# One of eight pairs of a fused attention and FFN kernel computes h with seven half-width block products

## The chip, the core and the metric

The kernel runs on one core of one Trainium2 chip. The metric is device time in microseconds (us) of one launch; lower is better. The engines are named as the profile names them: PE (matrix products; PEld are its weight loads), DVE and ACT (elementwise work), SP (which issues the DMAs here), POOL (idle here). Each engine takes its instructions strictly in the order of its own queue, so an instruction that waits holds up everything queued behind it on its engine.

## The reference

```python
def _attn_ref(q, k, v, tau):                     # q, k, v: (4, 6080, 256)
    qn = q / (norm(q, axis=1, keepdims=True) + 1e-06)
    kn = k / (norm(k, axis=1, keepdims=True) + 1e-06)
    s = kn.transpose(0, 2, 1) @ qn / tau         # (4, 256, 256): over channels
    s = s - s.max(-1, keepdims=True)
    a = exp(s)
    a /= a.sum(-1, keepdims=True) + 1e-09
    return v @ a

def _moe_ref(x, w_in, w_out):                    # x: (24320, 256), w_in: (256, 2048), w_out: (2048, 256)
    h = maximum(x @ w_in, 0.0)
    return h * h @ w_out
```

The output is `_moe_ref` of the attention's output, reshaped to 24320 tokens.

## The kernel before, in words

**What is computed.** The attention matrix `a` of a batch is only 256x256, so the kernel folds it into the weights: `W = a @ w_in`, once per batch, and then `h = relu(v W)`, squares it and multiplies with `w_out`. Every fp32 operand of a product is split into a high and a low float32r part (`..._hi` by a copy on ACT, `..._lo` by a subtraction on DVE), and each product is three: hi·hi, hi·lo, lo·hi.

**Tiles and steps.** A batch has 12 blocks of tokens, ten of 512 and two of 480 (`blocks`, line 75). A block has 16 steps, one for each 128 hidden columns (f), and two steps make a pair r (8 pairs). `first_product` (line 574) makes one step's h: six products of 512 columns into a bank of `ps_h` (three banks, line 98), and ACT evicts it through Relu into half of the tile `x`. After the odd step ACT squares `x` in place (`squares_and_sums`, line 598).

**The second product by seven.** For all blocks but the first two and the last, `h² @ w_out` uses the Strassen-Winograd scheme: over a pair and the two halves of the tokens it needs 7 block products of 256 columns (times 3 parts, 21 matmuls) in place of 8. It costs sums: three DVE operations on `x` (`x<-x`, 512, 256 and 256 elements) and two more slices in `g_hi`/`g_lo`, which hold the seven operands' parts: 768 elements of plain `x` (in `squares_and_sums`) and 1024 elements of sums (`parts_of_sums`, line 611, one step later). `g_hi` is ACT's, `g_lo` is DVE's. PE uses pair r's parts two pairs later (LAG, line 793): 9 matmuls in the even step (the 768-element parts), 12 in the odd step (`SEVEN`, line 641). When a block's eighth pair is through, ACT copies the results out of `ps_o` (`o<-ps_o`), and `combine` (line 681) adds them up on DVE at the next block's steps 5, 7 and 9.

**What runs beside it.** v of the next block is loaded (`load_v`), and split on ACT at step 6 and on DVE at step 8. The attention of the next batch runs as a generator (`attention`, line 370), one piece per step: a chunk of q and k is split in one even step (`qk_hi`, `qk_lo`), squared and added up in the next (`qk`, `acc`), and its products follow on PE (`gram`). It is skipped in steps 2 and 3 of a block (line 815). Its softmax and the new W (`softmax_and_W`, line 402) follow.

**Order.** The main loop (lines 795 to 843) writes out each step by hand: first product, generators in even steps, `parts_of_sums`, `squares_and_sums`, a piece of `combine`, second product, v's loads and splits, generators in odd steps. `InProgramOrder` keeps that order on each engine, so every instruction shows line 27 in the profile and has to be told by its tiles.

Of the kernel before, what the change touches and what calls it, by code (L numbers as in the profile page):

```python
# [30 lines left out]
def kernel(  # L31
# [25 lines left out]
    P = 128  # L57
# [7 lines left out]
    FPG = GRP // P  # L65
    J = 2
# [167 lines left out]
    now = {"part": 0}  # L234
    HEAD = 5
    QK_BUFS = 2
# [69 lines left out]
    def start_first(b=0):  # L306
# [7 lines left out]
        def load(c):  # L314
            if c == g.n:
                grams[1] = Gram(1)
            if c < g.n:
                g.load(c, FAST_TAGS[c % len(FAST_TAGS)])
            elif c < total and B > 1:
                grams[1].load(c - g.n, raw=room[:, c - g.n] if c - g.n < HEAD - 1 else None)  # L320
# [80 lines left out]

    def softmax_and_W(b):
# [49 lines left out]
        ps_b = ps_h.tile([P, T], F32, tag="h", name=f"ps_b{b}")  # L452
# [17 lines left out]
        ps_t = ps_h.tile([P, T], F32, tag="h", name=f"ps_t{b}")  # L470
# [6 lines left out]
        eT_hi = pool.tile([P, NC, C], F32R, tag="eT_hi", name=f"eT_hi{b}", bufs=1)  # L477
        eT_lo = pool.tile([P, NC, C], F32R, tag="eT_lo", name=f"eT_lo{b}", bufs=1)
# [5 lines left out]
        for g in range(NG):  # L484
# [54 lines left out]
            yield  # L539

# [16 lines left out]
    def once(f, *args):  # L557
        f(*args)
        yield

    def split_v_lo(b, n):
# [3 lines left out]
        vector.tensor_sub(V[b, n][2][:, :, :tn], raw[:, :, :tn], hi[:, :, :tn].bitcast(F32))  # L565

# [6 lines left out]

    def first_product(b, n, f):
        tn = blocks[n][1]
# [22 lines left out]
    def squares_and_sums(b, n, r):  # L598
# [3 lines left out]
        scalar.activation(x[:, 0:4, :], x[:, 0:4, :], AF.Square)  # L602
# [192 lines left out]
    for i in range(len(steps) + 2 * LAG):  # L795
        part = now["part"] = i % 2
        if i < len(steps):
# [26 lines left out]
        if part == 1 and i // 2 < len(pairs):  # L824
            squares_and_sums(*pairs[i // 2])
# [3 lines left out]
        if i >= 2 * LAG:  # L829
            second_product(*pairs[i // 2 - LAG], part)  # L830
        if i < len(steps):
            at_hi, at_lo = (None, None) if at == 0 else (12, 13) if at == 1 else (6, 8)
# [4 lines left out]
            if f == at_lo and at + 1 < len(order):  # L837
                split_v_lo(*order[at + 1])
                if at + 2 < len(order):
                    load_v(*order[at + 2])  # L840
        if i >= PAIR and part:
# [29 lines left out]
```

## Time and profile before

| what | value |
|---|---|
| time, median of 3 runs (range) | 2218.08 us (2217.61 to 2218.21) |
| the profiled execution's own time | 2217.84 us |
| its span | 2216.1 us |
| PE's granted clock | 1.000 |
| DMA, mean over the span | 57 GB/s |

The span is the time from the first to the last instruction of the profiled execution; 1.7 us of the execution's time lie around it. A "busy" PE is a model: matmuls overlap in the records, so their rate is read from the distance between starts. A row of the timeline gives start, duration, engine, operation, tiles (out<-in), the shape, how many equal ones were merged, and in brackets how long the engine stood idle before it and what released it.

### The profile page before, as it was taken

How to read it: one execution, taken by the hardware profiler on the slowest of the kernel's cores; microseconds unless marked ns; L12 is line 12 of the kernel's file. 1: busy time of each engine (PE TensorE's matmuls, PEld its weight loads, DVE VectorE, ACT ScalarE, POOL GpSimd, SP SyncE). 2: the span in 40 equal slices, each digit the busy share in tenths (PEclk: the TensorE clock that was granted, in tenths of full speed). 3: DMA queues.
4: the chain of work that ended last, by engine and by line, in shares of the span. 5: the costliest groups of instructions: out<-in, count | busy, mean ns of one | idle time of the engine just before them, and what ended most of it. 6: DMA issues, size and time to landing. Idle time of an engine off the chain costs nothing.

```text
span 2216.1 us, 34362 instructions
## 1 busy us (share of the span) xinstructions
PE 2204.7 (99%) x13740; PEld 1980.2 (89%) x13740; DVE 1760.9 (79%) x2470; ACT 1844.3 (83%) x2294; POOL 0.7 (0%) x6
## 2 busy tenths in 40 slices
PE   9999999999999999999999999999999999999999
PEld 7788999989989999988998999998899888888898
DVE  7878888888778888878767888887877777777773
ACT  5788888888788888888878888888887888888885
POOL 0000000000000000000000000000000000000000
PEclk9999999999999999999999999999999999999999
DMA  9511122101111122110121222110102010010000
GB/s 341 179 67 48 61 71 61 55 20 36 60 66 58 60 68 65 61 41 22 36 76 48 64 67 71 58 53 22 38 20 76 21 37 20 22 37 20 22 26 18
DMA packets 76495, 126.99 MB, mean 57 GB/s; under 512 B 7728, under 2 KB 35120, under 8 KB 76336
## 3 DMA queue, kind: packets, MB, share of 16 engines
q1 hardware_dynamic: 76336, 124.81, 17.2%
q8 instruction: 107, 1.75, 0.3%
q14 instruction: 52, 0.43, 0.1%
HBM read 95.68 MB, written 29.10 MB: 56 GB/s over the span
## 4 chain that ended last, share of the span: by engine, by line
PE 96%; DVE 1%; ACT 1%; DMA 1%; SPq 0%; issue 0%; DVEq 0%; ACTq 0%
PE ps_h L27 47%; PE ps_o L27 42%; PE gram L27 5%; PE ps_w L27 2%; DVE acc L27 1%; DMA qk<-in_k 1%; DMA qk<-in_q 0%; ACT x L27 0%; PE ps_n L27 0%; DVE g_lo L27 0%; DVE dec_m L27 0%; ACT g_hi L27 0%; DVE x L27 0%; ACT sq L27 0%; SPq L263 0%
## 5 line engine op out<-in xcount | busy, mean ns | idle before, releaser
L27 DVE TENSOR_TENSOR g_lo<-x,g_hi 128x768 fp32r<-128x768 f32 (+2 forms) x744 | 804.1, 1081 | 95.3 <-ACT g_hi L27 94.6
L27 DVE TENSOR_TENSOR x<-x 128x256 f32<-128x256 f32 (+3 forms) x1080 | 550.9, 510 | 277.6 <-ACT x L27 252.3
L27 ACT CAST g_hi<-x 128x768 fp32r<-128x768 f32 (+2 forms) x744 | 697.4, 937 | 25.3 <-DVE x L27 12.7
L27 ACT ACTIVATE x<-ps_h 128x512 f32<-128x512 f32 (+1 forms) x768 | 456.4, 594 | 290.6 <-PE ps_h L27 269.8
L27 PE MATMUL ps_h<-v_hi,w_hi 128*128 128x512 f32 (+1 forms) x1536 | 478.5, 393 | 0.0
L27 PE MATMUL ps_h<-v_hi,w_lo 128*128 128x512 f32 (+1 forms) x1536 | 477.6, 391 | 0.0
L27 PE MATMUL ps_h<-v_lo,w_hi 128*128 128x512 f32 (+1 forms) x1536 | 474.8, 390 | 0.0
L27 ACT ACTIVATE x<-x 128x1024 f32<-128x1024 f32 (+1 forms) x384 | 404.5, 1053 | 11.9
L27 PE MATMUL ps_o<-g_lo,wS_hi 128*128 128x256 f32 (+1 forms) x1440 | 401.7, 279 | 0.0
L27 PE MATMUL ps_o<-g_hi,wS_lo 128*128 128x256 f32 (+1 forms) x1440 | 401.2, 279 | 0.0
L27 PE MATMUL ps_o<-g_hi,wS_hi 128*128 128x256 f32 (+1 forms) x1440 | 400.4, 278 | 0.0
L27 PEld LDWEIGHTS ps_h<-v_lo,w_hi 128*128 128x128 f32 x1536 | 287.9, 187 | 64.9
L27 PEld LDWEIGHTS ps_h<-v_hi,w_lo 128*128 128x128 f32 x1536 | 288.5, 188 | 62.0
L27 PE MATMUL ps_o<-g_hi,wo_hi 128*128 128x256 f32 (+3 forms) x1176 | 330.8, 288 | 1.0 <-ACT g_hi L27 1.0
L27 PE MATMUL ps_o<-g_hi,wo_lo 128*128 128x256 f32 (+3 forms) x1176 | 330.8, 288 | 0.0
L27 PE MATMUL ps_o<-g_lo,wo_hi 128*128 128x256 f32 (+3 forms) x1176 | 330.5, 288 | 0.1
L27 PEld LDWEIGHTS ps_o<-g_lo,wS_hi 128*128 128x128 f32 x1440 | 271.0, 188 | 15.7
L27 PEld LDWEIGHTS ps_o<-g_hi,wS_hi 128*128 128x128 f32 x1440 | 270.3, 188 | 15.5
L27 PEld LDWEIGHTS ps_o<-g_hi,wS_lo 128*128 128x128 f32 x1440 | 270.6, 188 | 0.0
L27 PEld LDWEIGHTS ps_h<-v_hi,w_hi 128*128 128x128 f32 x1536 | 239.0, 188 | 5.2
L27 PEld LDWEIGHTS ps_o<-g_hi,wo_hi 128*128 128x128 f32 x1176 | 221.5, 188 | 17.7 <-ACT g_hi L27 1.4
L27 PEld LDWEIGHTS ps_o<-g_lo,wo_hi 128*128 128x128 f32 x1176 | 220.8, 188 | 16.7 <-DVE g_lo L27 0.5
(87 smaller groups left out, 1669.2 us busy)
## 6 DMA issues: line engine op xcount, KB each, us to landing
qk<-in_k SPq DMA_DIRECT2D x87, 256.0 KB, 2.8
qk<-in_q SPq DMA_DIRECT2D x87, 256.0 KB, 3.0
v<-in_vT SPq DMA_DIRECT2D x40, 512.0 KB, 3.7
out_T<-o SPq DMA_DIRECT2D x152, 128.0 KB, 1.7
wi_hi<-wi_kept SPq DMA_DIRECT2D x12, 512.0 KB, 3.2
wi_lo<-wi_kept SPq DMA_DIRECT2D x12, 512.0 KB, 4.1
w_raw<-in_w_in SPq DMA_DIRECT2D x4, 1024.0 KB, 6.1
w_raw<-in_w_out SPq DMA_DIRECT2D x4, 1024.0 KB, 5.4
```

Of the source, the lines that this page charges most:

```text
L27: return lambda *args, **kwargs: self.tc.keep_in_program_order(issue(*args, **kwargs))
```

## The change

Pair r = 5 (steps 10 and 11) of every block from the fourth on in batch 0, and from the second on in batches 1 to 3 (42 pairs in all), computes h by the same scheme of seven block products, each of half the tokens: 21 matmuls of 256 columns in place of 12 of 512.

- Step 10 makes four of the seven into two banks, `one` and `two` of `ps_h`; ACT copies two of them out (P1, P5), and DVE makes U2 = `one` + P1, adds U2 to both halves of `two` in PSUM, and makes the third sum `x3` = `two` + P5. Step 11 makes the other three products on top of these banks, and ACT evicts: Relu of `x3`, of `one`, of `two`. In the built program the first of the three (into `one`) waits for U2, the other two (into `two`) wait for `x3`; the copy P1 waits until the tile `x` is free, that is for the 1024-element `g_lo` of pair 3.
- In step 11 the second product is issued ahead of the first product. The sums and 768-element parts of pair 4 (`sums_and_parts`) move from step 9 to step 10, behind the new DVE operations.
- The generators are also skipped in step 10. So the attention's pieces for ACT and DVE run in six even steps of a block (0, 4, 6, 8, 12, 14) where it was seven.
- v's sums (three DVE operations, `v_sums`) are made in step 0, ahead of pair 0's sums; their parts in step 3 (ACT, `vS_hi`) and step 6 (DVE, `vS_lo`). The split of the next block's v moves from steps 6 and 8 to 9 and 12, and its load to step 0.
- W's sums for pair 5 are made once per batch (`sums_of_W`, six DVE operations, one ACT copy).
- For memory: w_in's parts share the tag of the q/k chunks (`qk`), eT shares `qk_hi`, and for batches 1 to 3 the softmax's `ps_b` and `ps_t` use the gram's bank in place of one of `ps_h`.

```diff
--- before.py
+++ after.py
...
+    def small_psum(b, name):
+
+        if b:
+            return ps_g.tile([P, NC, C], F32, tag="gram", name=f"{name}{b}").rearrange("p a b -> p (a b)")
+        return ps_h.tile([P, T], F32, tag="h", name=f"{name}{b}")
...
-        ps_b = ps_h.tile([P, T], F32, tag="h", name=f"ps_b{b}")
+        ps_b = small_psum(b, "ps_b")
...
+    SEVEN_FIRST, FIRST = (5,), 3
+    WS = {}
...
+    def sums_of_W(b, r):
+
+        while now["dec"]:
+            yield
+        f0 = 2 * (r % PPG) * P
+        hi, lo = (w[:, :, f0 : f0 + 2 * P].bitcast(F32) for w in W[b, r // PPG])
+        room = pool.tile([P, 2, NC, 2 * P], F32, tag="dec", name=f"w{b}_{r}", bufs=1)
+        w = room[:, 0]
+        S = room[:, 1].rearrange("p j (i m) -> p (j i) m", i=2)
+        vector.tensor_add(w, hi, lo)
+        A11, A12, A21, A22 = (w[:, j, i * P : (i + 1) * P] for i in range(2) for j in range(2))
+        S1, S2, S3, S4 = (S[:, i] for i in range(4))
+        vector.tensor_add(S1, A21, A22)
+        vector.tensor_sub(S3, A11, A21)
+        vector.tensor_sub(S2, S1, A11)
+        vector.tensor_sub(S4, A12, S2)
+        WS[b, r] = [pool.tile([P, 4, P], F32R, tag=f"WS{r}_{p}", name=f"WS_{p}{b}_{r}", bufs=1) for p in ("hi", "lo")]
+        scalar.copy(WS[b, r][0], S)
+        vector.tensor_sub(WS[b, r][1], S, WS[b, r][0].bitcast(F32))
+        yield
...
+    def sums_of_v(b, n):
+        tn = blocks[n][1]
+        half = tn // 2
+        raw = V[b, n][0]
+        S = pool.tile([P, 4, half], F32, tag="dec", name=f"v_sums{b}_{n}", bufs=1)
+        VS[b, n] = [pool.tile([P, 4, half], F32R, tag=f"vS_{p}", name=f"vS_{p}{b}_{n}", bufs=1) for p in ("hi", "lo")]
+        VS[b, n].append(S)
+        B21, B22 = raw[:, 1, 0:half], raw[:, 1, half:tn]
+        vector.tensor_sub(S[:, 0:3:2, :], raw[:, :, half:tn], raw[:, 0, :tn].rearrange("p (k t) -> p k t", k=2))
+        vector.tensor_sub(S[:, 1, :], B22, S[:, 0, :])
+        vector.tensor_sub(S[:, 3, :], B21, S[:, 1, :])
+        now["dec"] = True
+
+    def sums_of_v_hi(b, n):
+        scalar.copy(VS[b, n][0], VS[b, n][2])
+
+    def sums_of_v_lo(b, n):
+        hi, lo, S = VS[b, n]
+        vector.tensor_sub(lo, S, hi.bitcast(F32))
+        now["dec"] = False
...
+        if part == 0:
+            x = X[b, n, r] = pool.tile([P, 8, half], F32, tag="x", name=f"x{b}_{n}_{r}")
+            one, two = H[b, n, r] = [
+                ps_h.tile([P, 2, T // 2], F32, tag="h", name=f"ps_h{b}_{n}_{r}_{i}")[:, :, :half] for i in range(2)
+            ]
+            product(one[:, 0], "A11", "B11", start=True)
+            product(one[:, 1], "S2", "T2", stop=True)
+            product(two[:, 0], "S1", "T1", start=True)
+            product(two[:, 1], "S3", "T3")
+            P1, P5, U2 = (x[:, i, :] for i in (4, 5, 6))
+            scalar.copy(P1, one[:, 0])
+            scalar.copy(P5, two[:, 0])
+            vector.tensor_add(U2, one[:, 1], P1)
+            vector.tensor_add(two, two, x[:, 6:7, :].broadcast_to([P, 2, half]))
+            vector.tensor_add(x[:, 3, :], two[:, 1], P5)
+        else:
+            one, two = H.pop((b, n, r))
+            x = X[b, n, r]
+            product(one[:, 0], "A12", "B21", stop=True)
+            product(two[:, 0], "S4", "B22")
+            product(two[:, 1], "A22", "T4", stop=True)
+            scalar.activation(x[:, 3, :], x[:, 3, :], AF.Relu)
+            scalar.activation(x[:, 0, :], one[:, 0], AF.Relu)
+            scalar.activation(x[:, 1:3, :], two, AF.Relu)
...
-    def squares_and_sums(b, n, r):
+    def squares(b, n, r):
+        x = X[b, n, r]
+        scalar.activation(x[:, 0:4, :], x[:, 0:4, :], AF.Square)
+
+    def sums_and_parts(b, n, r):
...
+        chained, chain_next = (j < len(steps) and first_by_seven(*steps[j]) for j in (i, i + 1))
+        if chained and part:
+            second_product(*pairs[i // 2 - LAG], part)
...
-        if i >= PAIR and steps[min(i, len(steps) - 1)][2] in (2 * LAG - 2, 2 * LAG - 1):
+        if i >= PAIR and (chained and part == 0 or steps[min(i, len(steps) - 1)][2] in (2 * LAG - 2, 2 * LAG - 1)):
             gens = ()
         if i < PAIR or part == 0:
             for gen in gens:
                 next(gen, None)
+        if chained and part == 0:
+            sums_and_parts(*pairs[i // 2 - 1])
         if part == 0 and 0 <= i // 2 - 1 < len(pairs):
             parts_of_sums(*pairs[i // 2 - 1])
         if i in steps_of_W:
             next(first)
         if part == 1 and i // 2 < len(pairs):
-            squares_and_sums(*pairs[i // 2])
+            squares(*pairs[i // 2])
+            if not chain_next:
+                sums_and_parts(*pairs[i // 2])
         if part and late_work:
             if next(late_work[0], "end") == "end":
                 late_work.pop(0)
-        if i >= 2 * LAG:
+        if i >= 2 * LAG and not (chained and part):
             second_product(*pairs[i // 2 - LAG], part)
         if i < len(steps):
-            at_hi, at_lo = (None, None) if at == 0 else (12, 13) if at == 1 else (6, 8)
+            at_hi, at_lo = (None, None) if at == 0 else (12, 13) if at == 1 else (9, 12)
             if i == 2 and len(order) > 2:
                 load_v(*order[2])
             if f == at_hi and at + 1 < len(order):
                 split_v_hi(*order[at + 1])
             if f == at_lo and at + 1 < len(order):
                 split_v_lo(*order[at + 1])
-                if at + 2 < len(order):
+                if at == 1 and at + 2 < len(order):
                     load_v(*order[at + 2])
+            if at > FIRST - 1:
+                if f == 0 and has_sums(b, n):
+                    sums_of_v(b, n)
+                if f == 0 and at + 1 < len(order):
+                    load_v(*order[at + 1])
+                if f == 3 and has_sums(b, n):
+                    sums_of_v_hi(b, n)
+                if f == 6 and has_sums(b, n):
+                    sums_of_v_lo(b, n)
+            if i in (26, 28):
+                next(first, None)```

DVE's queue around pair 5 of block 5 in batch 1, before (the name x1_5_4 is tile `x` of batch 1, block 5, pair 4; g_lo likewise):

```order
L27 TENSOR_TENSOR g_lo1_5_3_8336<-x1_5_3_8308,g_hi1_5_3_8335 128x1024
L27 TENSOR_TENSOR v_lo1_6_8388<-v1_6_7912,v_hi1_6_8325 128x1024
L27 TENSOR_TENSOR x1_5_4_8364<-x1_5_4_8364 128x512
L27 TENSOR_TENSOR x1_5_4_8364<-x1_5_4_8364 128x256 x2
L27 TENSOR_TENSOR g_lo1_5_4_8401<-x1_5_4_8364,g_hi1_5_4_8400 128x768
L27 TENSOR_TENSOR o1_4_8202<-o1_4_8202 128x256
L27 TENSOR_TENSOR o1_4_8202<-o1_4_8202 128x2x256
L27 TENSOR_TENSOR qk_lo2_17_8442<-qk2_17_8244,qk_hi2_17_8441 128x1024
L27 TENSOR_TENSOR g_lo1_5_4_8401<-x1_5_4_8364,g_hi1_5_4_8400 128x1024
L27 TENSOR_TENSOR x1_5_5_8439<-x1_5_5_8439 128x512
```

The same place now (ps_h1_5_5_0 is bank `one`, ps_h1_5_5_1 bank `two`):

```order
L27 TENSOR_TENSOR g_lo1_5_3_8608<-x1_5_3_8573,g_hi1_5_3_8607 128x1024
L27 TENSOR_TENSOR o1_4_8479<-o1_4_8479 128x256
L27 TENSOR_TENSOR o1_4_8479<-o1_4_8479 128x2x256
L27 TENSOR_TENSOR x1_5_5_8687<-ps_h1_5_5_0_8688,x1_5_5_8687 128x256
L27 TENSOR_TENSOR ps_h1_5_5_1_8689<-ps_h1_5_5_1_8689,x1_5_5_8687 128x512
L27 TENSOR_TENSOR x1_5_5_8687<-ps_h1_5_5_1_8689,x1_5_5_8687 128x256
L27 TENSOR_TENSOR x1_5_4_8641<-x1_5_4_8641 128x512
L27 TENSOR_TENSOR x1_5_4_8641<-x1_5_4_8641 128x256 x2
L27 TENSOR_TENSOR g_lo1_5_4_8708<-x1_5_4_8641,g_hi1_5_4_8707 128x768
L27 TENSOR_TENSOR g_lo1_5_4_8708<-x1_5_4_8641,g_hi1_5_4_8707 128x1024
L27 TENSOR_TENSOR x1_5_5_8687<-x1_5_5_8687 128x512
```

The three new operations stand ahead of pair 4's sums, and two pieces of combine ahead of them; `v_lo` is gone from here.

ACT's queue from the eviction of step 3 to that of step 5 of the same block, before:

```order
L27 ACTIVATE x1_5_1_8189<-ps_h1_5_3_8204 128x512
L27 ACTIVATE x1_5_1_8189<-x1_5_1_8189 128x1024
L27 CAST g_hi1_5_1_8212<-x1_5_1_8189 128x768
L27 COPY o1_4_8202<-ps_o1_4_1_7804 128x1024
L27 ACTIVATE x1_5_2_8240<-ps_h1_5_4_8233 128x512
L27 ACTIVATE qk2_15_7959<-qk2_15_7959 128x1024
L27 CAST g_hi1_5_1_8212<-x1_5_1_8189 128x1024
L27 ACTIVATE x1_5_2_8240<-ps_h1_5_5_8265 128x512
```

The same stretch of ACT's queue now:

```order
L27 ACTIVATE x1_5_1_8466<-ps_h1_5_3_8481 128x512
L27 ACTIVATE x1_5_1_8466<-x1_5_1_8466 128x1024
L27 CAST g_hi1_5_1_8490<-x1_5_1_8466 128x768
L27 COPY o1_4_8479<-ps_o1_4_1_8063 128x1024
L27 CAST vS_hi1_5_8418<-v_sums1_5_8417 128x1024
L27 ACTIVATE x1_5_2_8518<-ps_h1_5_4_8511 128x512
L27 CAST qk_hi2_13_8520<-qk2_13_8278 128x1024
L27 CAST g_hi1_5_1_8490<-x1_5_1_8466 128x1024
L27 ACTIVATE x1_5_2_8518<-ps_h1_5_5_8536 128x512
```

`vS_hi` is put in ahead of the eviction of step 4.

More of the change, by code (lines that the diff above doesn't have):

```diff
@@ L319, in load @@
             elif c < total and B > 1:
-                grams[1].load(c - g.n, raw=room[:, c - g.n] if c - g.n < HEAD - 1 else None)
+                last = pool.tile([P, 2, J, C], F32, tag="vS_lo", name="qk_head", bufs=1) if c == total - 1 else None
+                grams[1].load(c - g.n, raw=room[:, c - g.n] if last is None else last)
         for c in range(AHEAD):
```

48 lines of the change are left out of this document (36 added, 12 removed).

## The prediction

> **What bounds the kernel now.** I read the page first: the engines' busy time and the chain that ended last.
>
> ```profile
> PE 2204.7 (99%) x13740; PEld 1980.2 (89%) x13740; DVE 1760.9 (79%) x2470; ACT 1844.3 (83%) x2294; POOL 0.7 (0%) x6
> PE 96%; DVE 1%; ACT 1%; DMA 1%; SPq 0%; issue 0%; DVEq 0%; ACTq 0%
> ```
>
> PE is the bound: the chain lies on it for 96% of the span. The list of waits says the same, since ACT's longest wait in total is for PE:
>
> ```profile
> ACT x L27 <- PE ps_h L27: 269.8, 462, 4.2
> ```
>
> Those 269.8 us are the only reserve that ACT has, and shares of the whole span hide how it is spread. So next come windows of one block each: one beside three chunks of attention, one without attention, one of 480 tokens, and the last block of batch 1, which makes the next W.
>
> ```profile
> core 0: us, PE busy (x) PEld busy (x) DVE busy (x) ACT busy (x) POOL busy (x), PEclk, DMA share, GB/s
> 205.00:251.20 46.20, 46.20 (x302) 41.91 (x302) 39.33 (x52) 41.16 (x50) 0.00 (x0) 1.00 0.18 58
> 1833.80:1875.70 41.90, 41.90 (x267) 37.63 (x266) 32.28 (x47) 35.34 (x44) 0.00 (x0) 1.00 0.08 26
> 1071.30:1111.10 39.80, 39.80 (x266) 36.99 (x265) 30.85 (x47) 33.71 (x43) 0.00 (x0) 1.00 0.09 27
> 1111.10:1158.00 46.90, 46.90 (x296) 42.67 (x296) 33.65 (x52) 35.94 (x48) 0.00 (x0) 1.00 0.20 67
> ```
>
> PE never pauses in them, but beside attention ACT is already busy for 41.2 of 46.2 us and DVE for 39.3.
>
> **What PE gains.** Half-width products are only worth it if they take half the time. PE's timeline, for 512 and 256 columns and for 480 and 240:
>
> ```profile
> 1000.80 0.63 PE L27 MATMUL ps_h<-v_hi,w_hi 128*128 128x512 f32 x2
> ...
> 1002.20 0.28 PE L27 MATMUL ps_o<-g_hi,wo_hi 128*128 128x256 f32 x1
> ...
> 1003.25 0.62 PE L27 MATMUL ps_h<-v_hi,w_hi 128*128 128x512 f32 x2
> ...
> 1089.80 0.59 PE L27 MATMUL ps_h<-v_hi,w_hi 128*128 128x480 f32 x2
> ...
> 1091.09 0.27 PE L27 MATMUL ps_o<-g_hi,wo_hi 128*128 128x240 f32 x1
> ...
> 1092.10 0.59 PE L27 MATMUL ps_h<-v_hi,w_hi 128*128 128x480 f32 x2
> ```
>
> Six products of 512 take 1002.20 - 1000.80 = 1.40 us, 0.233 each; the nine of 256 behind them take 1.05, 0.117 each. Twelve wide ones are 2.80, twenty-one narrow ones 2.45 to 2.46: 0.34 us gained in a pair. At 480 tokens it is 0.215 and 0.112, so 2.58 - 2.36 = 0.22. Of the 42 pairs 34 lie in blocks of 512 and 8 in blocks of 480: 34 x 0.34 + 8 x 0.22 = 13.3 us. No product is added elsewhere on PE.
>
> [...]
>
> **What DVE and ACT pay, step by step.** For each kind of instruction I take the distance from its start to the next one's, in a stretch where the queue never ran dry. DVE:
>
> ```profile
> 1364.35 0.69 DVE L27 TENSOR_TENSOR o<-o 128x512 f32<-128x512 f32 x1
> 1364.95 1.22 DVE L27 TENSOR_TENSOR acc<-acc,qk 128x1024 f32<-128x1024 f32 x1
> ...
> 1367.73 1.61 DVE L27 TENSOR_TENSOR x<-x 128x512 f32<-128x512 f32 x3 [0.43 <-ACT x L27]
> 1369.26 0.95 DVE L27 TENSOR_TENSOR g_lo<-x,g_hi 128x768 fp32r<-128x768 f32 x1
> 1370.13 0.88 DVE L27 TENSOR_TENSOR o<-o 128x256 f32<-128x256 f32 x2
> 1370.92 1.22 DVE L27 TENSOR_TENSOR qk_lo<-qk,qk_hi 128x1024 fp32r<-128x1024 f32 x1
> 1372.06 1.22 DVE L27 TENSOR_TENSOR g_lo<-x,g_hi 128x1024 fp32r<-128x1024 f32 x1
> 1373.19 1.22 DVE L27 TENSOR_TENSOR v_lo<-v,v_hi 128x1024 fp32r<-128x1024 f32 x1
> ...
> 1376.72 1.14 DVE L27 TENSOR_TENSOR o<-o 128x256 f32<-128x256 f32 x2
> 1377.78 1.22 DVE L27 TENSOR_TENSOR acc<-acc,qk 128x1024 f32<-128x1024 f32 x1
> ```
>
> So: a pair's three sums 1.53, `g_lo` of 768 elements 0.87, anything of 1024 elements 1.14, combine 0.60, 0.79 and 1.06 in its three pieces. ACT:
>
> ```profile
> 1352.52 1.04 ACT L27 CAST g_hi<-x 128x1024 fp32r<-128x1024 f32 x1
> 1353.45 0.80 ACT L27 COPY o<-ps_o 128x768 f32<-128x768 f32 x1
> 1354.46 0.60 ACT L27 ACTIVATE x<-ps_h 128x512 f32<-128x512 f32 x1 [0.20 <-PE ps_h L27]
> 1355.09 1.06 ACT L27 ACTIVATE x<-x 128x1024 f32<-128x1024 f32 x1
> 1356.20 0.83 ACT L27 CAST g_hi<-x 128x768 fp32r<-128x768 f32 x1
> 1356.94 1.01 ACT L27 COPY o<-ps_o 128x1024 f32<-128x1024 f32 x1
> 1357.84 0.60 ACT L27 ACTIVATE x<-ps_h 128x512 f32<-128x512 f32 x1
> 1358.33 1.05 ACT L27 CAST qk_hi<-qk 128x1024 fp32r<-128x1024 f32 x1
> 1359.27 1.06 ACT L27 CAST g_hi<-x 128x1024 fp32r<-128x1024 f32 x1
> 1360.22 0.60 ACT L27 ACTIVATE x<-ps_h 128x512 f32<-128x512 f32 x1
> 1360.85 1.06 ACT L27 ACTIVATE x<-x 128x1024 f32<-128x1024 f32 x1
> ```
>
> So: eviction 0.49 or, where the square waits for it, 0.63; square 1.10; 768 elements 0.74; 1024 elements 0.94; the results' copies 0.70 and 0.90. For the new small operations the groups give:
>
> ```profile
> L27 ACT ACTIVATE x<-ps_h 128x512 f32<-128x512 f32 x640 | 383.2, 599 | 224.2 <-PE ps_h L27 204.8 <-DVE g_lo L27 11.4 <-DVE v_lo L27 1.8
> L27 DVE TENSOR_TENSOR x<-x 128x256 f32<-128x256 f32 x608 | 258.5, 425 | 20.8
> L27 DVE TENSOR_TENSOR x<-x 128x512 f32<-128x512 f32 x304 | 210.0, 691 | 196.9 <-ACT x L27 196.4
> L27 DVE TENSOR_TENSOR s<-s,ps_b 128x512 f32<-128x512 f32 x4 | 2.7, 680 | 0.4 <-PE ps_b L27 0.4
> ```
>
> A DVE operation of 512 elements costs the same from PSUM (680 ns) as from SBUF (691). U2, the sum into `two`, and `x3` depend on each other: 0.43 + 0.69 + 0.43 and some 0.03 between them, 1.60 us. No row shows DVE writing PSUM; I take 0.69 for that one and keep up to twice that as the upper end. On ACT a Relu of 256 elements takes some 0.39 (0.60 less 256 elements at 0.85 ns, the slope from 512 to 1024 above), 0.30 to the next start.
>
> In one block that is, on DVE, 1.60 + 1.53 (`v_sums`) + 1.14 (`vS_lo`), on ACT some 2 us. By busy time it fits. But the work is a chain that passes from one queue to the other, so I follow it through one block beside attention, from the end of `x3` (time 0) to the next one's, taking what each queue holds in program order:
>
> 1. DVE makes pair 4's sums (done 1.53), only then can ACT make its 1024-element `g_hi`, and behind that in ACT's queue stand the Relus of `x3`, `one`, `two` and the square: 0.94 + 0.30 + 0.30 + 0.63 + 1.10. Pair 5's sums start at 4.8.
> 2. DVE is then never idle: three pairs' sums and 768-element parts (3 x 2.40), seven operations of 1024 elements (three `g_lo`, `v_lo`, two `acc`, one `qk_lo`: 7.98), `v_sums` 1.53: 16.7. Pair 0's sums start at 21.5 and give their last result at 23.1.
> 3. ACT's 1024-element `g_hi` of pair 0 has waited for that, and what stands behind it follows: `g_hi` 0.94, copy 0.70, eviction 0.63, square 1.10, 768 elements 0.74, copy 0.90, the new `vS_hi` 0.94, eviction 0.49, `qk_hi` 0.94, `g_hi` 0.94, eviction 0.63, square 1.10: 10.05. Pair 2's sums start at 33.2.
> 4. DVE again without a gap: two pairs' sums and 768-element parts 4.80, combine 2.45, five of 1024 elements (`acc`, `g_lo`, `vS_lo`, `qk_lo`, `g_lo`) 5.70, the three new operations 1.60: 14.55. `x3` ends at **47.7**.
>
> PE needs for the same block 46.2 - 0.34 = 45.9 us. `x3` is what the last six products of step 11 wait for, and PE takes its queue in order, so the block lasts 47.7: 1.8 us of waiting in every such pair. In the first one of a batch, where DVE still starts on time, the same steps give a wait of 0.5.
>
> Without attention there is no `acc`, `qk_lo`, `qk_hi`: part 1 is 4.8; in part 2 DVE now waits for ACT between pairs (sums 1.6, `g_hi` 0.94, eviction 0.63, square 1.1, 4.3 a pair; with `v_lo` and `v_sums` between them 14.7, and 1.6 to the last sum); part 3 is 9.1; part 4 is 14.55 - 2.28 = 12.3. That is **42.5** against PE's 41.9 - 0.34 = 41.6: 0.9 us of waiting. At 480 tokens DVE's busy time is 30.85/32.28 = 0.956 of that, so some 40.6 against 39.6: 1.0.
>
> The 42 pairs: 22 beside attention (3 first ones 0.5 = 1.5; 19 at 1.8 = 34.2); 10 in blocks of 512 without attention at 0.9 = 9.0, one more that starts half-way on time, 0.6, and the first of batch 3 with none; 5 of 480 at 1.0 = 5.0; and three that lie in the blocks of 46.9 us, where W's products give PE 7 us of other work, with none. Sum 50.3 us.
>
> **The rest** has one answer. W's sums are about 3 us on DVE three times outside the blocks above, and once in batch 0's first blocks; the 768-element parts are ready some 3.5 us ahead of PE there (they wait two pairs), so nothing. v's load now has steps 0 to 9 for its landing. The shared tags are free before they are asked for: w_in's reload comes after the last chunk. `ps_b` and `ps_t` in the gram's bank take pressure off `ps_h`, where no PE wait is shown now: nothing either way, at most 1 us.
>
> **Sum.** 2217.8 - 13.3 + 50.3 = 2254.8 for the profiled execution, which lies 0.2 us under the median; the forecast for the median is **2255**, 1.7% slower.
>
> **The rivals.**
>
> - *Nothing waits, faster.* If both chains are shorter than PE's block, by 1.8 of 47.7 us (4%) and 0.9 of 42.5 (2%), the pairs gain their 13.3: 2204.8. For it: the three banks of `ps_h` and LAG let the queues run behind for some microseconds, and PE waits nowhere now. Against it: the distances are measured, and a lag that comes back in every block is not absorbed by buffers. Chance 0.18.
> - *Only beside attention.* If part 1 or 3 is a microsecond shorter than I have it, blocks without attention just hold: 2217.8 - 13.3 + 36 = 2240.5. Chance 0.17.
> - *PSUM is dearer on DVE.* If the sum into `two` takes twice as long, `x3` comes 0.7 later in some 36 pairs: up to 2280, middle 2267. Chance 0.13.
> - *Gain and wait cancel.* A quarter of the waits, 13 us: within 0.2%, about 4.4 us and about what a measurement of this kernel can tell from no change. Chance 0.05.
>
> [...]
>
> **How the numbers follow.** The forecast's case, both chains binding, has 0.47. An error of 0.5 us in a block's chain moves its result by 18 us, so its own range is 2237 to 2273. Slower by over 0.2%: 0.47 + 0.17 + 0.13 = 0.77; same 0.05; faster 0.18. The range leaves out the case without waits and the far end of the dear PSUM: 2216 to 2277.
>
> **What would show it.** Right: PE idle before `ps_h` products, released by DVE `x`, once in a block, 1 to 2 us beside attention and under 1 us in batch 3; ACT's waits for PE much below 269.8 us; blocks beside attention near 47.7 us, batch 3's near 42.5. Wrong: blocks of 41.6 us in batch 3 and no wait on PE (the first rival), or a sum into `two` of well over 0.7 us (the third). If PE waited mostly for `g_lo` or for W at a batch's border, the mechanism would be another.

## The result, and the profile after

The changed kernel takes 2274.3 us (median of 4 runs, 2273.4 to 2275.4), the kernel before beside it 2217.85 (2217.6 to 2218.2): a ratio of 1.0255, 95% interval 1.0237 to 1.0272, so 56 us slower. The forecast was 2255, its range 2216 to 2277. The profiled execution of the changed kernel takes 2274.5 us, its span is 2272.7.

From the page of the changed kernel, the engines and the chain that ended last:

```profile
PE 2222.5 (98%) x14118; PEld 1993.4 (88%) x14118; DVE 1926.0 (85%) x2788; ACT 1869.1 (82%) x2466; POOL 0.7 (0%) x6
DVE 47%; ACT 28%; PE 19%; issue 4%; DMA 1%; DVEq 0%; SPq 0%; ACTq 0%
```

The "busy" shares hardly tell the two kernels apart (PE 99% and 98%). The chain does: 96% on PE before, now 75% on DVE and ACT. The list of waits of the changed kernel (us in total, times, longest) says the same from the other side:

```profile
ACT g_hi L27 <- DVE x L27: 244.3, 209, 3.7
...
ACT x L27 <- PE ps_h L27: 76.6, 96, 4.2
...
PE ps_h L27 <- DVE x L27: 21.0, 37, 1.2
```

ACT's reserve, its wait for PE, went from 269.8 to 76.6 us, and ACT now waits for DVE's sums instead. PE waits for DVE's `x` 37 times, 35 of them for `x3` and two for U2. The same four kinds of block as before, in windows of the changed kernel: beside attention, without, the first of 480 tokens in batch 1, and the block behind it, in which half of the next W is made. Blocks are named (batch, block) from here on; these are (2,5), (3,3), (1,10) and (1,11):

```profile
core 0: us, PE busy (x) PEld busy (x) DVE busy (x) ACT busy (x) POOL busy (x), PEclk, DMA share, GB/s
1427.90:1475.60 47.70, 46.74 (x311) 42.29 (x310) 42.53 (x60) 40.97 (x54) 0.00 (x0) 1.00 0.18 56
1885.30:1928.00 42.70, 42.15 (x274) 37.81 (x273) 36.17 (x54) 35.39 (x49) 0.00 (x0) 1.00 0.08 25
1100.80:1143.30 42.50, 41.80 (x284) 38.43 (x283) 37.21 (x60) 34.75 (x53) 0.00 (x0) 1.00 0.08 25
1143.30:1189.40 46.10, 44.69 (x291) 40.64 (x290) 38.58 (x60) 36.31 (x52) 0.00 (x0) 1.00 0.24 80
```

No engine is full in any of them: of DVE and ACT, DVE is the busier and works 42.5 of 47.7 us. Yet every steady block beside attention takes the same 47.7. The prediction's walk can be laid over the timeline of DVE, from the `x3` of block (2,4) (the first row) to that of block (2,5) (the last):

```profile
1411.81 0.42 DVE L27 TENSOR_TENSOR x<-ps_h,x 128x256 f32<-128x256 f32 x1
...
1417.03 1.61 DVE L27 TENSOR_TENSOR x<-x 128x512 f32<-128x512 f32 x3 [0.94 <-ACT x L27]
...
1433.67 1.60 DVE L27 TENSOR_TENSOR x<-x 128x512 f32<-128x512 f32 x3
...
1445.38 1.61 DVE L27 TENSOR_TENSOR x<-x 128x512 f32<-128x512 f32 x3 [0.18 <-ACT x L27]
...
1459.55 0.42 DVE L27 TENSOR_TENSOR x<-ps_h,x 128x256 f32<-128x256 f32 x1
```

`x3` ends at 1412.23. Pair 5's sums start 4.80 later (the walk had 4.8), pair 0's sums end 18.24 after that (18.3), pair 2's sums start 10.11 later (10.05), and `x3` ends 14.59 later (14.55): 47.74, as worked out. Without attention, in batch 3 from the `x3` that ends at 1870.39 to the one at 1913.13, the same four stretches take 4.81, 16.31, 9.16 and 12.46 us (the walk had 4.8, 16.3, 9.1 and 12.3). On PE the end of it is this row, the first of the products into `two` that wait for `x3`:

```profile
1460.12 0.36 PE L27 MATMUL ps_h<-v_hi,WS_hi 128*128 128x256 f32 x1 [0.74 <-DVE x L27]
```

Lengths of blocks of five kernels, from ACT's first eviction in a block to its first in the next (worked out from the timelines); the last three columns are experiments below:

| block | before | after | sums in step 2 | turn in step 10 | all placed anew, W spread |
|---|---|---|---|---|---|
| (2,0), second half of W | 47.19 | 48.09 | 48.09 | 48.11 | 45.92 |
| (2,1), first with the pair | 46.23 | 47.13 | 46.60 | 48.54 | 47.93 |
| (2,4) | 47.68 | 47.74 | 46.58 | 48.90 | 47.17 |
| (2,5) | 46.23 | 47.74 | 46.60 | 48.89 | 46.46 |
| (2,8) | 43.03 | 46.68 | 45.50 | 47.97 | 44.42 |
| (2,9), softmax | 41.55 | 45.30 | 44.86 | 43.77 | 42.02 |
| (2,10), 480 tokens | 39.86 | 42.44 | 41.37 | 40.93 | 39.50 |
| (2,11) | 46.89 | 46.15 | 45.77 | 45.70 | 46.18 |
| batch 2 in all | 546.3 | 562.3 | 551.7 | 567.0 | 545.5 |
| (3,3), no attention | 41.87 | 42.73 | 41.68 | 42.74 | 41.58 |
| (3,10), 480, no attention | 39.86 | 40.90 | 39.82 | 40.91 | 39.63 |

(In the kernel before, blocks alternate because 38 and 46 of gram's products fall into them; in the changed one a steady block has 36, and where attention gets its turn in step 10 back, 42.)

### The profile page after: what moved, and what is told of

Its sections match the earlier page's. It is cut to its first block, busy times and chain, and to the rows that moved or that the text cites. A ratio compares the mean times of both kernels' runs of the same rounds, so it can differ in the third digit from the quotient of the medians.

```text
span 2272.7 us, 35657 instructions
## 1 busy us (share of the span) xinstructions
PE 2222.5 (98%) x14118; PEld 1993.4 (88%) x14118; DVE 1926.0 (85%) x2788; ACT 1869.1 (82%) x2466; POOL 0.7 (0%) x6
## 4 chain that ended last, share of the span: by engine, by line
DVE 47%; ACT 28%; PE 19%; issue 4%; DMA 1%; DVEq 0%; SPq 0%; ACTq 0%
DVE x L27 18%; ACT x L27 13%; DVE g_lo L27 13%; PE ps_h L27 9%; PE ps_o L27 8%; ACT g_hi L27 8%; DVE acc L27 4%; ACT o L27 3%; DVE v_sums L27 2%; DVE qk_lo L27 2%; DVE v_lo L27 2%; DVE vS_lo L27 2%; DVE o L27 2%; PE ps_w L27 2%; ACT vS_hi L27 2%
## 5 line engine op out<-in xcount | busy, mean ns | idle before, releaser
L27 ACT CAST g_hi<-x 128x768 fp32r<-128x768 f32 (+2 forms) x744 | 697.9, 938 | 254.8 <-DVE x L27 244.3
L27 DVE TENSOR_TENSOR g_lo<-x,g_hi 128x768 fp32r<-128x768 f32 (+2 forms) x744 | 803.8, 1080 | 99.3 <-ACT g_hi L27 98.6
L27 DVE TENSOR_TENSOR x<-x 128x256 f32<-128x256 f32 (+3 forms) x1080 | 549.6, 509 | 149.9 <-ACT x L27 124.3
L27 ACT ACTIVATE x<-ps_h 128x512 f32<-128x512 f32 (+2 forms) x768 | 439.5, 578 | 74.3 <-PE ps_h L27 72.0
L27 PE MATMUL ps_h<-v_hi,w_hi 128*128 128x512 f32 (+3 forms) x1452 | 451.8, 388 | 5.8 <-ACT x L27 3.8
L27 PE MATMUL ps_h<-v_hi,w_lo 128*128 128x512 f32 (+3 forms) x1452 | 448.8, 385 | 0.0
L27 PE MATMUL ps_h<-v_lo,w_hi 128*128 128x512 f32 (+3 forms) x1452 | 446.9, 384 | 0.0
L27 ACT ACTIVATE x<-x 128x1024 f32<-128x1024 f32 (+3 forms) x426 | 421.5, 989 | 12.2 <-DVE x L27 0.3
L27 PE MATMUL ps_o<-g_hi,wS_hi 128*128 128x256 f32 (+1 forms) x1440 | 401.9, 279 | 4.7 <-ACT o L27 4.6
L27 PE MATMUL ps_o<-g_lo,wS_hi 128*128 128x256 f32 (+1 forms) x1440 | 403.5, 280 | 0.2
L27 PE MATMUL ps_o<-g_hi,wS_lo 128*128 128x256 f32 (+1 forms) x1440 | 401.1, 279 | 0.0
L27 PE MATMUL ps_o<-g_hi,wo_hi 128*128 128x256 f32 (+3 forms) x1176 | 332.2, 289 | 1.2 <-ACT g_hi L27 0.9
L27 PE MATMUL ps_o<-g_lo,wo_hi 128*128 128x256 f32 (+3 forms) x1176 | 332.9, 290 | 0.4 <-DVE g_lo L27 0.3
L27 PE MATMUL ps_o<-g_hi,wo_lo 128*128 128x256 f32 (+3 forms) x1176 | 330.8, 288 | 0.0
L27 PEld LDWEIGHTS ps_h<-v_lo,w_hi 128*128 128x128 f32 x1452 | 272.6, 188 | 57.9
L27 PEld LDWEIGHTS ps_h<-v_hi,w_lo 128*128 128x128 f32 x1452 | 273.0, 188 | 55.4
L27 PEld LDWEIGHTS ps_o<-g_hi,wS_hi 128*128 128x128 f32 x1440 | 270.4, 188 | 23.4 <-ACT o L27 10.3
L27 PEld LDWEIGHTS ps_o<-g_lo,wS_hi 128*128 128x128 f32 x1440 | 271.0, 188 | 16.2 <-DVE g_lo L27 2.8
L27 PEld LDWEIGHTS ps_o<-g_hi,wS_lo 128*128 128x128 f32 x1440 | 270.8, 188 | 0.0
L27 PEld LDWEIGHTS ps_h<-v_hi,w_hi 128*128 128x128 f32 x1452 | 228.5, 188 | 12.3 <-ACT x L27 5.0
L27 PEld LDWEIGHTS ps_o<-g_lo,wo_hi 128*128 128x128 f32 x1176 | 221.1, 188 | 18.0 <-DVE g_lo L27 3.1
L27 PEld LDWEIGHTS ps_o<-g_hi,wo_hi 128*128 128x128 f32 x1176 | 221.5, 188 | 16.7 <-ACT g_hi L27 1.4
```

The source lines that it names most:

```text
L27: return lambda *args, **kwargs: self.tc.keep_in_program_order(issue(*args, **kwargs))
```

## The experiments

Theory A is the prediction's: a closed chain through DVE's and ACT's queues, taken in order, sets the block. Its rivals: the pair's own hand-over (ACT's copies, the sum into PSUM, Relu) makes PE late wherever the other work stands, or there is simply too much work. Each experiment starts from the changed kernel and ran beside the kernel before (2219.1 us beside the first four, 2218.0 to 2218.2 beside the others). The times are of one execution each, except for the two runs with all work placed anew, which have 11.

**The sums alone.** The sums of v and W, their parts and the moved splits of v stay; no pair is made by seven. Attention's turn in step 10 and the places of pair 4's sums and of the second product in step 11 hang on the same test, so they too are as in the kernel before (38 and 46 gram products in its blocks).

```diff
-        return has_sums(b, n) and f // 2 in SEVEN_FIRST
+        return False
```

> The changed kernel with all its sums of v and W, their parts, and every moved step, but with all pairs of h computed as before (no pair by seven). Theory A (a chain that passes between DVE's and ACT's queues and closes through the third sum x3 is longer than PE's block): without x3 the chain is not closed, PE paces the block again, and DVE's 2.7 us and ACT's 0.9 us more in a block hide. What stays is W's sums, up to 7 us: 2217 to 2227 us. Theory B (only the pair itself: 21 matmuls are too short a cover for the copies, U2 and x3, whatever the queues hold elsewhere): 2218. Theory C (the moved splits of v, the skipped generators, the shared tags and the sums cost by themselves): 2250 or more.

Measured 2224.0. Of the 5 us over the kernel before, 2.9 lie ahead of block (0,2) (it starts at 161.7 us in this execution, at 158.8 in the kernel before and at 158.5 to 160.2 in the other runs), in code that the edit doesn't touch; in this execution the granted clock was 0.51 from 49.2 to 52.6 us (0.999 over the whole span, 1.000 in the kernel before beside it). So the sums, as work, cost 2 to 5 us. That they become dear with the pair that closes the chain is what A says of this; as the edit also gives back attention's turn and the old places, this run alone doesn't show it.

**The pair without v's sums.** v's sums and their parts are left out; the pair reads plain parts of v in their place, so v's sums are missing from the result. PE's products are the same in number and shape.

> The changed kernel without v's sums and their parts: the pair by seven multiplies with plain parts of v in their place, so PE's, and the pair's own DVE and ACT work, are the same and its output is not the reference's. Theory A: the chain loses 1.53 (the sums), 0.94 (vS_hi) and 1.14 (vS_lo): 47.7 to 44.1 us beside attention and 42.5 to 38.9 without, both under PE's 45.9 and 41.6, so PE waits no more and the gain of 13 us shows, less W's sums: 2205 to 2216 us. Theory B: the pair is as it was, the waits stay: 2260 or more. Theory C: 2260 or more, since the other edits stay.

Measured 2214.9. Windows of block (2,5) and of (3,3):

```profile
1388.90:1434.80 45.90, 45.90 (x311) 42.14 (x310) 40.23 (x56) 40.16 (x53) 0.00 (x0) 1.00 0.19 58
1834.60:1876.10 41.50, 41.50 (x274) 37.81 (x273) 33.75 (x49) 34.83 (x47) 0.00 (x0) 1.00 0.08 26
```

PE never pauses: the hand-over by itself costs nothing here, and PE's need is 45.9 and 41.5 us, as the prediction had it (45.9, 41.6). The rival of the hand-over falls for these blocks.

**The same sums, in step 2.** v's sums and the next v's load move from step 0 to step 2, so out of the stretch from pair 5's to pair 0's sums, which DVE bounds, into the next one, where it waits for ACT.

```diff
-                if f == 0 and has_sums(b, n):
+                if f == 2 and has_sums(b, n):
                     sums_of_v(b, n)
-                if f == 0 and at + 1 < len(order):
+                if f == 2 and at + 1 < len(order):
```

> The same work as in the changed kernel, only that v's three sums (and the load of the next v behind them) are made in step 2, behind pair 0's sums and parts, in place of step 0, ahead of them. Theory A: the sums leave the stretch in which ACT waits for pair 0's sums, and go to one in which DVE waits for ACT (1.1 and 1.8 us idle in the walk): chains of some 46.2 and 41.1 us, nearly PE's 45.9 and 41.6: 2208 to 2225 us. A rival of A (DVE simply has too much work in a block, in whatever order): no change, 2265 to 2276. Theory B: no change, 2265 to 2276.

Measured 2232.0: 42 of the 56 us come back though no work is less. It is 7 us above A's range, and the same two blocks show why:

```profile
1402.60:1449.20 46.60, 46.16 (x311) 42.22 (x310) 42.48 (x60) 41.09 (x54) 0.00 (x0) 1.00 0.18 57
1851.30:1893.00 41.70, 41.70 (x275) 37.84 (x274) 36.23 (x54) 35.45 (x49) 0.00 (x0) 1.00 0.08 26
```

Without attention PE is now full; beside attention 0.4 us of waiting remain. In their new place the sums fill idle time of DVE, but push pair 1's sums back by 0.4 us (they start 5.42 us after pair 0's, where the changed kernel has 5.01). DVE's busy time is what it was in the slow kernel (42.48 against 42.53). That is the clearest answer to "too much work".

**v's sums and `vS_lo` on POOL.** `vector` becomes `pool_engine` in these four operations.

> v's three sums and the low part vS_lo run on POOL, which is idle, in place of DVE; ACT still makes vS_hi. Theory A: DVE's part of the chain loses 1.53 + 1.14: 45.0 and 39.8 us, under PE's 45.9 and 41.6: 2206 to 2220 us, if POOL has the parts ready by step 10 and does not slow DVE down, for which no run here has a row yet. Theory B: the waits stay, 2260 or more.

Measured 2290.7, slower than the change itself: A missed, and its condition that POOL doesn't slow DVE down did not hold, so this run doesn't decide between A and B. POOL's timeline in block (2,4), and DVE's in the same microseconds:

```profile
1401.75 2.41 POOL L27 TENSOR_TENSOR vS_lo<-v_sums,vS_hi 128x1024 fp32r<-128x1024 f32 x1 [40.65 <-ACT vS_hi L27]
1404.24 2.15 POOL L27 TENSOR_TENSOR v_sums<-v 128x512 f32<-128x512 f32 x1
1406.47 2.75 POOL L27 TENSOR_TENSOR v_sums<-v,v_sums 128x256 f32<-128x256 f32 x2
```

```profile
1403.14 2.10 DVE L27 TENSOR_TENSOR qk_lo<-qk,qk_hi 128x1024 fp32r<-128x1024 f32 x1 [1.68 <-ACT qk_hi L27]
1405.17 2.31 DVE L27 TENSOR_TENSOR g_lo<-x,g_hi 128x1024 fp32r<-128x1024 f32 x1
1407.40 2.57 DVE L27 TENSOR_TENSOR x<-x 128x512 f32<-128x512 f32 x3
```

DVE's operations of 1024 elements take 1.22 us in this run where POOL is idle, and 2.10 and 2.31 here, the three sums 1.60 and here 2.57: 2.94 us lost in a block, against 2.67 (1.53 + 1.14) taken off DVE. `qk_lo` started under POOL's `vS_lo` and ended 1.08 us after it. What holds DVE up beside POOL is not shown.

**Pair 4's copy behind the Relus.** No work changes. On ACT `g_hi` of pair 4's last four slots comes behind pair 5's square, on DVE its subtraction behind pair 5's sums.

```diff
-        if part == 0 and 0 <= i // 2 - 1 < len(pairs):
+        if part == 0 and not (chained and by_seven(*steps[i][:2])) and 0 <= i // 2 - 1 < len(pairs):
             parts_of_sums(*pairs[i // 2 - 1])
...
             squares(*pairs[i // 2])
+            lo_of_4 = parts_hi(*pairs[i // 2 - 1]) if chained and by_seven(b, n) else None
             if not chain_next:
-                sums_and_parts(*pairs[i // 2])
+                sums_and_parts(*pairs[i // 2], lo_of_4)
```

> The changed kernel with one edit, no work added or left out: pair 4's copy of 1024 elements (g_hi of its last four slots) stands on ACT behind the three Relus and the square of pair 5 instead of ahead of them, and its subtraction on DVE behind pair 5's sums. Theory A (a closed chain through the two queues in order sets the block): the part of the chain from x3 to pair 5's sums falls from 4.8 to about 2.4 us, the chain from 47.7 to 45.3 us, below PE's 45.9, so blocks beside attention take 45.9 to 46.3 and those of batch 3 41.6; the whole 2215 to 2235. Theory B (the pair's own hand-over, copy to sum to Relu, costs PE its 1.2 us wherever the parts stand): blocks stay at 47.5 to 47.8, the whole 2268 to 2278. Theory C (DVE and ACT are simply too full beside attention): the same as B.

Measured 2271.4, in the range of B and C: my theory, as I had sharpened it, missed; blocks beside attention take 47.83. DVE's timeline around a pair, from `x3` on, and ACT's rows of step 12's eviction, beside attention and, the last one, in batch 3:

```profile
1411.09 0.42 DVE L27 TENSOR_TENSOR x<-ps_h,x 128x256 f32<-128x256 f32 x1
...
1414.37 1.61 DVE L27 TENSOR_TENSOR x<-x 128x512 f32<-128x512 f32 x3 [0.47 <-ACT x L27]
1415.90 2.08 DVE L27 TENSOR_TENSOR g_lo<-x,g_hi 128x1024 fp32r<-128x1024 f32 x2
1418.78 1.22 DVE L27 TENSOR_TENSOR acc<-acc,qk 128x1024 f32<-128x1024 f32 x1 [0.80 <-ACT qk L27]
```

```profile
1417.21 0.60 ACT L27 ACTIVATE x<-ps_h 128x512 f32<-128x512 f32 x1 [1.20 <-PE ps_h L27]
1417.70 1.05 ACT L27 ACTIVATE qk<-qk 128x1024 f32<-128x1024 f32 x1
...
1916.78 0.60 ACT L27 ACTIVATE x<-ps_h 128x512 f32<-128x512 f32 x1 [1.20 <-DVE g_lo L27]
```

The link did get shorter: pair 5's sums start 2.86 us after `x3` instead of 4.80. But DVE's `acc` starts 7.27 after `x3`, where the changed kernel has 7.20 (1459.97 to 1467.17). It waits for ACT's square `qk`, and that for the eviction ahead of it, before which ACT stands idle for 1.20 us. The row names PE, but step 12's products had ended 3 us earlier. What the eviction waits for is tile `x`: it has two buffers, pair 6 takes the one of pair 4, and pair 4's 1024-element `g_lo`, the last to read it, is what the edit had moved behind pair 5's sums (the first of the two operations in the `g_lo` row). In all 37 places of this form the eviction starts 0.09 us after the end of that `g_lo`, while its distance from the end of PE's last product before it runs from 0.04 to 0.72, and in batch 3 the row itself names `g_lo`. So the edit made one link of the loop shorter and another longer; it is no evidence against A, and it doesn't tell A from B or C.

**W's sums spread.** From batch 1 on, W's sums take another tile, and ACT's copy and DVE's subtraction come a turn of the generator later each.

```diff
...
         vector.tensor_sub(S4, A12, S2)
+        if b:
+            yield
...
         scalar.copy(WS[b, r][0], S)
+        if b:
+            yield
```

> The changed kernel with one edit: in batches 1 to 3 the sums of W for pair 5 take another tile, and ACT's copy and DVE's subtraction that follow DVE's five operations are issued one step later each, where before all stood in one step. Theory A (W's sums are the term that was priced at nothing: ACT's copy waits 3.3 us in order behind DVE's five operations, and the block behind a new W grew by 2.35 us in batch 3): blocks (1,0), (2,0), (3,0) become 1.5 to 2.4 us shorter, the whole 2267 to 2270. Theory B (those blocks grew because work moved into them from the block before, which is 0.75 to 1.9 us shorter): nothing changes in the sum, 2272 to 2276.

Measured 2277.0, a microsecond above B's range. But the edit did not do what it was for: ACT still waits for W's sums.

```profile
ACT WS_hi L27 <- DVE w L27: 11.0, 4, 3.0
```

In the changed kernel the row reads 13.0, 4, 3.3. So this run alone decides nothing on W's term.

**Attention's turn in step 10 given back**, so seven even steps as before; and the same with the sums in step 2.

```diff
-        if i >= PAIR and (chained and part == 0 or steps[min(i, len(steps) - 1)][2] in (2 * LAG - 2, 2 * LAG - 1)):
+        if i >= PAIR and steps[min(i, len(steps) - 1)][2] in (2 * LAG - 2, 2 * LAG - 1):
```

> The changed kernel with one part undone: attention again gets its turn in step 10, so seven of a block's eight even steps as before, not six. Theory A (the growth of the blocks at a batch's border, (b,8) to (b,10) and (b,0), comes from attention ending later: its chunks, the softmax and W's products slide into the next blocks and PE waits there): the border blocks go back to within 1 us of before, blocks beside attention stay at 47.5 to 48, the whole 2252 to 2264. Theory B (that growth is W's and v's sums): nothing changes at the border, the whole 2272 to 2285, since the turn adds two copies of 1024 elements to the fullest stretch of the chain.

> Two edits on the changed kernel: v's sums and the next v's load in step 2, and attention's turn in step 10 given back. Pair 4's copy stays where the change put it. Theory A (both costs are separate: 42 us came back by the first edit, the border by the second): 2215 to 2222, about as before. Theory B (the turn in step 10 fills the stretch that the first edit had emptied): 2228 or more.

Measured 2283.1 and 2239.4: 8.8 more than the changed kernel and 7.4 more than the sums in step 2, B's side both times. Blocks (b,9) and (b,10) get shorter, as A had it for the border, but in the first of the two runs every steady block beside attention takes 48.9, in the second 47.4 to 47.8 instead of 46.6. B's reason holds: step 10 lies in the stretch that DVE bounds, and 42 gram products a block instead of 36 bring their DVE and ACT work into it. Leaving that turn out, one of the change's own parts, was a help.

**All of it placed anew.** The change's whole work, with each piece where its engine has room: v's sums in step 3 of the block before, `vS_hi` in its step 13, `vS_lo` in step 2, v loaded a block earlier, attention's turn in step 10 back, W's sums in another tile.

```diff
...
-                if f == 0 and has_sums(b, n):
-                    sums_of_v(b, n)
...
+                if f == 2 and has_sums(b, n):
                     sums_of_v_lo(b, n)
+                ahead = order[at + 1] if at + 1 < len(order) and has_sums(*order[at + 1]) else None
+                if f == 3 and ahead:
+                    sums_of_v(*ahead)
+                if f == 13 and ahead:
+                    sums_of_v_hi(*ahead)
```

> All of the changed kernel's work, placed anew: attention's turn in step 10 given back; the sums of v for a block are made in step 3 of the block before, their rounded part on ACT in step 13 of it, and the rest of 1024 elements on DVE in step 2 of the block itself; v is loaded a block earlier, W's sums take another tile. So v's sums lie in the stretch where DVE waits for ACT, none in the two stretches that DVE bounds. Theory A (the closed chain: 1.53 + 1.14 us leave the stretches that DVE bounds and 0.94 us the one that ACT bounds, so the chain falls from 47.7 to about 44 to 45 us, below PE's): PE bounds nearly every block, the whole 2204 to 2214, faster than before by 0.2 to 0.6%. Theory B (PE is late for a pair by seven whatever the order, by its hand-over from ACT to DVE and back): 0.5 us or more in each of 42 pairs remains, 2222 or more.

Measured 2220.9 (11 runs), 1.0012 times the kernel before, interval 1.0003 to 1.0021: 53 us less than the change, 7 above A's range, below B's. Blocks without attention take 41.58, 0.29 less than before, and PE waits for DVE's `x` 4 times (2.3 us in all), where the changed kernel had 37 (21.0): the hand-over needs no wait in the other pairs.

**The same with W's sums spread** as above.

> The run with all work placed anew, with one more edit: in batches 1 to 3 ACT's copy and DVE's subtraction behind W's sums come one turn later each. Theory A (with the turn in step 10 the blocks (b,0) and (b,1) are 1.6 us per batch shorter where W's sums are spread, as the two earlier runs with and without that edit show): 4 to 5 us less than the run before it, 2214 to 2218, within 0.2% of before. Theory B (as when the sums were spread alone, the time only moves into the next block): 2219 to 2224.

Measured 2215.25 (2214.8 to 2217.2, 11 runs; before 2218.0), ratio 0.9989, interval 0.9980 to 0.9998: faster than both kernels, if by little. Here the spreading works. ACT's wait for W's sums in the run before and in this one:

```profile
ACT WS_hi L27 <- DVE w L27: 11.7, 4, 2.9
```

```profile
ACT WS_hi L27 <- DVE w L27: 3.0, 1, 3.0
```

The one wait that is left is batch 0's, whose sums the edit doesn't spread. The chain that ended last in this run, and windows beside attention (two blocks), without it, and of 480 tokens:

```profile
PE 87%; DVE 8%; ACT 3%; issue 1%; DMA 1%; SPq 0%; DVEq 0%; ACTq 0%
```

```profile
1393.50:1440.00 46.50, 46.50 (x316) 42.74 (x315) 43.77 (x61) 41.94 (x56) 0.00 (x0) 1.00 0.20 62
1346.30:1393.50 47.20, 47.12 (x319) 43.13 (x318) 43.73 (x61) 42.12 (x55) 0.00 (x0) 1.00 0.21 63
1834.40:1876.00 41.60, 41.60 (x274) 37.89 (x274) 36.17 (x54) 35.87 (x49) 0.00 (x0) 1.00 0.09 26
1073.20:1112.70 39.50, 39.50 (x275) 37.04 (x273) 34.59 (x54) 34.20 (x49) 0.00 (x0) 1.00 0.09 28
```

PE bounds them all, with more DVE and ACT work inside a block (43.8 and 41.9 us) than in the slow kernel.

**Two mixtures** hold pair 4's late copy together with the sums in step 2 and W's spread sums, the second also attention's turn in step 10.

> Three edits on the changed kernel, no work left out: the Relus ahead of pair 4's copy, v's sums and the next v's load in step 2, W's sums spread over three steps. Theory A: with part 1 of the chain 2.4 us shorter and v's sums out of the stretch that DVE bounds, PE is never late for a pair by seven, and the whole comes to that of the kernel without v's sums or below it, 2206 to 2216, faster than before. Theory B (hand-over or fullness): 2225 or more.

> The three edits of the run before, and attention again gets a turn in step 10, so seven even steps of a block as in the kernel before instead of six: attention ends one to two blocks earlier. Theory A (the blocks 8 to 10 grew only because gram products moved into them, and the softmax now ends so late that PE waits 1.25 us for an eviction in block 11): the wait in block 11 goes, 3 to 5 us less than the run before. Theory B (the turn in step 10 puts a copy of 1024 elements on ACT and one on DVE just where the chain has the least room): blocks beside attention grow by 0.3 us or more, 5 to 15 us more than the run before.

Measured 2250.5 and 2237.0. The first is 18.5 slower than the sums in step 2 alone: with the chain out of the way the late copy brings a wait of its own, once in a block on PE, for pair 4's parts:

```profile
PE ps_o L27 <- DVE g_lo L27: 22.9, 38, 0.6
```

The second is 13.6 faster than the first, more than A had, while the same turn cost 7 to 9 us above. W's spreading works in it as in the last run (ACT's wait is 2.9 us, once) and not in the first; how much of the 13.6 is that was not separated.

## Why the prediction was right, and where its size was off

- **Direction and mechanism.** Right. The walk gave 47.7 and 42.5 us for the blocks with and without attention; measured 47.74 and 42.73. Moving 1.53 us out of a stretch that DVE bounds takes 42 us off, and the same work in other places makes PE the bound again. That the time lies inside the stated range is in part luck: the forecast's own case ended at 2273, and the range went on to 2277 only for a dearer PSUM, which didn't come.
- **PE's gain.** Forecast 0.34 us a pair; with PE full, 41.87 - 41.58 = 0.29, and 0.23 at 480 tokens (0.22). Over the 42 pairs some 12 us, not 13.3.
- **Where PE waits.** The prediction had all of a block's wait at `x3`, 1 to 2 us beside attention. By the row above it is 0.74 there. The rest of the 1.8 lies at other products that need something from the two late queues, beside attention `qk_lo`, in batch 3 ACT's copy of the results, in the blocks (b,11) an eviction of ACT's (the third row):

```profile
PE gram L27 <- DVE qk_lo L27: 7.0, 21, 0.8
PE ps_o L27 <- ACT o L27: 4.8, 12, 0.7
PE ps_h L27 <- ACT x L27: 3.8, 3, 1.3
```

  The loop sets how long the block is; PE meets the delay wherever it first asks.
- **The known waits** were a little small. A pair without attention waits 42.73 - 41.58 = 1.15 us (forecast 0.9), at 480 tokens 40.90 - 39.63 = 1.27 (1.0), a batch's first one 47.1 to 47.3 less 45.9, so 1.2 to 1.4 (0.5), a steady one 47.74 - 45.9 = 1.8 (1.8).
- **"The rest … nothing" was the step that failed.** By the forecast's own terms batch 2 should have grown by 11.5 us; it grew by 16.0. To place the waits I add up, on PE's timeline from block (0,2) on, what the distance from one matmul's start to the next one's exceeds the usual one of its width (0.233 us at 512 columns, 0.117 at 256), where it does so by more than 0.06. The changed kernel loses 72.0 us in this way and the kernel before 3.4; with the 12 us that PE gains this is the 56.6 by which it is slower. The forecast had 50.3. In the blocks (b,9) to (b,11) and the one behind them, twelve in all, where the softmax and W stand, it is 22.5 us where the forecast had 5.4 (0.6, twice 0.9, three times 1.0, else none); in all others 49.5 where it had 44.9. So 17 of the 19 us that were missing lie at the batches' borders.
- **What they are there** is known in part. With v's sums left out and the chain open, 11.5 us of border waits stay (1.4 in all other blocks), so half of them are no part of the steady chain: 4.3 for an eviction of ACT's in (b,11), 1.9 for `qk_lo` in (1,0) and (2,0), 1.8 for the softmax's `diag`. With the sums in step 2 the border has 15.5 us, and 9.9 when attention gets its turn in step 10 back, so the moved attention is one of the causes. Some 1.5 us of the 22.5 are not the change's: in this execution the granted clock was 0.51 for 3.4 us, in block (0,10), and PE's products came further apart there, those of 480 columns 0.40 us in place of 0.215 and those of 240 mostly 0.21 in place of 0.112.

```profile
566.20:569.60 3.40, 3.40 (x13) 2.98 (x13) 2.53 (x4) 2.75 (x5) 0.00 (x0) 0.51 0.02 5
```

  "About 3 us on DVE … outside the blocks above" was wrong for W's sums in that they also hold ACT for 3 us, in order: in batch 1 ACT stands idle for 3.34 us ahead of `WS_hi`, and the eviction queued behind that copy starts at 666.42 us, though its products had ended at 662.57. What this costs is not shown: the only waits of PE in (1,0), (2,0) and (3,0) are the two for `qk_lo`, and the 5.6 us between the last two runs (2220.9 - 2215.25) are not theirs alone. Batches 1 and 2 got 2.8 and 2.7 us shorter, but batch 3, where the same wait went, not at all; spreading the sums also moves attention's products ((2,0) has 4 of gram's instead of 12, (2,7) 30 instead of 24). Work as such the border's waits are not: with the same work placed anew batch 2 takes 545.5 us, less than the 546.3 before.
- **PSUM is dearer on DVE.** Wrong. The groups of the changed kernel:

```profile
L27 DVE TENSOR_TENSOR x<-ps_h,x 128x256 f32<-128x256 f32 x68 | 28.6, 421 | 1.6
L27 DVE TENSOR_TENSOR ps_h<-ps_h,x 128x512 f32<-128x512 f32 x34 | 23.8, 700 | 3.9 <-ACT g_hi L27 0.5
```

  421 and 700 ns, where the same kernel's `x<-x`, from SBUF to SBUF, takes 425 and 687.
- **Nothing waits; only beside attention.** Neither: blocks without attention waited 1.15 us each. `ps_b` and `ps_t` in the gram's bank, v's later load and the shared tags show no wait, as forecast; they were not undone one by one.

## What to carry to other kernels

Two engines that are each under 90% busy (DVE 85% and ACT 82% here) can still set the time, when their queues hand work to each other in a loop: write down the loop from one result to the same result a block later, and compare its length with the bound engine's need. What an extra operation costs is then decided by the stretch of the loop it stands in, not by its duration: the same 1.53 us made the kernel 42 us slower in one step than two steps later. Before moving an operation to shorten a link, ask which buffers it keeps: one that is released later can be the next link, as `x` was with the late copy, where ACT stood idle for 1.20 us. And look at every place where the new work stands outside the steady block; here 17 of the 19 us that the forecast missed lay there.

## What the runs showed of the hardware

Subtractions on POOL, by the groups of that run:

```profile
L27 POOL TENSOR_TENSOR v_sums<-v,v_sums 128x256 f32<-128x256 f32 x68 | 85.0, 1251 | 5.3
L27 POOL TENSOR_TENSOR vS_lo<-v_sums,vS_hi 128x1024 fp32r<-128x1024 f32 x34 | 81.9, 2408 | 1285.8 <-ACT vS_hi L27 1285.8
L27 POOL TENSOR_TENSOR v_sums<-v 128x512 f32<-128x512 f32 x34 | 69.9, 2057 | 379.4 <-DVE WS_lo L27 219.0 <-DMA v<-in_vT 158.0
```

They take 2.41, 2.06 and 1.25 us where DVE takes 1.22, 0.68 and 0.43 in the changed kernel. DVE's own operations took longer beside them, 2.10, 2.31 and 2.57 us in place of 1.22, 1.22 and 1.60: 2.67 us of a block moved off DVE cost it 2.94 in the block shown. DVE adds into PSUM in place, 512 elements in 0.70 us, where SBUF to SBUF it takes 0.69.
